# Attention and MLP mixer in one kernel: unread TensorE products in three places, token mixing in bunches, a cast moved, the last product group halved

## The chip, the cores and the metric

The kernel runs on one core of one Trainium2 chip. The metric is the device time of one execution in microseconds (us), as the median of several runs. A second source is one profiled execution of the same kernel, with its own time and its span from the first to the last instruction. The engines are TensorE (PE in the profile; its weight loads are PEld), VectorE (DVE), ScalarE (ACT), GpSimd (POOL) and SyncE (SP), which issues most of the DMAs.

## What is computed

The reference normalises queries and keys, does softmax attention over 8 batches of 12 heads (448 positions, 64 per head), joins the heads to x of 8 x 448 x 768, and sends x through an MLP mixer: first mixing along the positions, then along the channels.

```
q_n, k_n = q / (|q| + 1e-6), k / (|k| + 1e-6)
attn = softmax(q_n @ k_n.T / tau);  x = heads joined(attn @ v)
h = relu(x.T @ w_tok1) @ w_tok2          # 448 -> 256 -> 448
u = x + h.T
out = u + relu(u @ w_ch1) @ w_ch2        # 768 -> 1536 -> 768
```

## The kernel before

**Pairs of heads and slots.** The work is cut into 48 pairs of heads, six for each batch. Slot i computes the scores and exponentials of pair i, the attention output of pair i-1, and prepares pairs i+1 to i+3. The scores come in two groups of two (`score(i, 0)`, `score(i, 1)`, line 252); each of the four products of 2 x 448 columns is read by one exponential on ScalarE (line 268). `pv` (line 271) makes the attention output pO in two parts (three row tiles, then the last one), and VectorE normalises it into x16 (lines 288 and 289). Squares of q and k and their scaling to unit length run on POOL (lines 180 and 213). `norm_sum` (line 189) sums the squares on VectorE, `norm_root` (193) takes the root on ScalarE, and `norm_rec` (198) the reciprocal on VectorE.

**Opening.** The first 13 slots (`opening`, line 476) transpose q and k with TensorE (`tpose_pe`, line 233), and VectorE copies the result out (line 248). Later slots (`slot`, line 526) use a DMA for that (`tpose_dma`). The prologue (lines 443 to 471) loads, scales and transposes pair 0. In slots 1 and 2 `w2_cast` (line 138) casts one half each of w_tok2 on ScalarE; its load is issued in the prologue. Batch 0's token mixing is done pair by pair in the opening (`tok1_pair`, `tok2_pair`, `u_pair`, lines 346 to 373).

**Mixer.** For each later batch b, `mixer(b)` returns lists of jobs: `tok1` (four jobs, line 308) with a relu on ScalarE; `tok2` (two jobs for each row tile i, line 320), whose VectorE adds (line 335) give u32; after the second job of a row tile, the tile is cast to u16 (line 339 on VectorE for odd i, line 341 on ScalarE for even i) and transposed by a DMA into uT; `ch1` (twelve jobs, line 375) with a relu on ScalarE (381); `ch2` (two jobs for each row tile, line 384), with an add on VectorE (392) and stores. Even batches have three row tiles (i = 0 to 2), odd ones four (i = 3 to 6).

**Order of the work.** Each engine runs its instructions in program order. `fill` (line 434) is called five times in a slot; each call adds a fixed credit and takes jobs off the front of a list while the credit lasts. Every six slots the list is loaded again (lines 581 to 585): token mixing of the batch just finished is merged with the ch2 jobs held over from the batch before (one ch2 after every four token jobs, then the last three), then comes ch1; the new ch2 jobs are held. For the last batch (mixer 7) there are no slots left, and the list runs straight through.

**PSUM.** All products but the scores take their banks from one ring of four (`ps`, line 65). A product waits until the reader of the bank four allocations before is done.

Of the kernel before, what the change touches and what calls it, by code (L numbers as in the profile page):

```python
# [9 lines left out]
FP32 = mybir.dt.float32  # L10
FP16 = mybir.dt.float16
AF = mybir.ActivationFunctionType
ALU = mybir.AluOpType
# [10 lines left out]
def kernel(  # L24
# [136 lines left out]
    def load(i, names="qkv"):  # L161
        b, pj = pairs[i]
        for nm in names:
            t = ld.tile([P, 2, NCH, E], FP32, name=f"{nm}l", tag=f"{nm}l")
            nc.sync.dma_start(
                out=t[:].rearrange("p g c e -> p g (c e)"),
                in_=src[nm][b, 2 * pj:2 * pj + 2].rearrange("g (p c) e -> p g (c e)", c=NCH))
            st_[i][nm] = t
# [64 lines left out]
    def tpose_pe(i, act=False, between=None):  # L233
        s = st_[i]
        s["T"] = att.tile([128, 2, S], FP16, name="qkT", tag="qkT")
        for js in ((slice(0, 1), slice(1, 2)) if act else (BOTH,)):
# [12 lines left out]
            if between and not js.start:  # L249
                between()  # L250

    def score(i, g):

        s = st_[i]
        if g == 0:
            s["p"] = att.tile([P, NCH, 2, S], FP16, name="pE", tag="pE")
            s["pS"] = {}
        for c in (2 * g, 2 * g + 1):
            pS = pss.tile([P, 2, 512], FP32, name="pS", tag="pS")
            for h in range(2):  # L260
                nc.tensor.matmul(pS[:, h, 0:S],  # L261
                                 s["T"][64 * h:64 * h + 64, 1, c * P:(c + 1) * P],
                                 s["T"][64 * h:64 * h + 64, 0, :], start=True, stop=True)
            s["pS"][c] = pS
# [6 lines left out]
    def pv(i, half):  # L271
        b, pj = pairs[i]
        s = st_[i]
        xt = x16[b // 2]
        d0 = 2 * pj * E
        ts = (3,) if half else (0, 1, 2)
        pO = ps.tile([128, len(ts), 2, E + 1], FP32, name="pO", tag="ps")
        for n, t in enumerate(ts):
            c0 = 128 * t if t < 3 else S - 128
            for h in range(2):  # L280
                for c in range(NCH):
                    nc.tensor.matmul(pO[:, n, h, :], s["p"][:, c, h, c0:c0 + 128],  # L282
                                     s["v16"][:, NCH * h + c, 0:E + 1],
                                     start=(c == 0), stop=(c == NCH - 1))
        m0, hp = (64, 64 * (b % 2)) if half else (0, 0)
        nr, t0 = 128 - m0, (3 if half else 4 * (b % 2))
        rec = att.tile([128, len(ts), 2], FP32, name="rec", tag=f"rec{half}")
        nc.vector.reciprocal(out=rec[m0:128], in_=pO[m0:128, :, :, E])  # L288
        nc.vector.tensor_tensor(  # L289
            out=xt[hp:hp + nr, t0:t0 + len(ts), d0:d0 + 2 * E].rearrange(  # L290
                "p t (h e) -> p t h e", h=2),
            in0=pO[m0:128, :, :, 0:E], in1=_bcast_free(rec[m0:128], E), op=ALU.mult)
# [4 lines left out]
    def mixer(b):  # L297
# [22 lines left out]
        def tok2(i, dh):  # L320
            def job():
                pU = ps.tile([128, DH], FP32, name="pU", tag="ps")
                for tt in range(TT):
                    if i != 3:
                        c0 = 128 * (i % 4)
                        nc.tensor.matmul(pU[:], w2t[:, tt, c0:c0 + 128],  # L326
                                         r16[b][:, tt, dh * DH:(dh + 1) * DH],
                                         start=(tt == 0), stop=(tt == TT - 1))
                    else:
                        for h in range(2):  # L330
                            nc.tensor.matmul(pU[64 * h:64 * h + 64], w2t[:, tt, S - 64:S],
                                             r16[2 * g + h][:, tt, dh * DH:(dh + 1) * DH],
                                             start=(tt == 0), stop=(tt == TT - 1))
                cols = slice(dh * DH, (dh + 1) * DH)
                nc.vector.tensor_tensor(out=u32[:, i - t0, cols], in0=pU[:], in1=xt[:, i, cols],  # L335
                                        op=ALU.add)
                if dh == NDH - 1:
                    if i % 2:
                        nc.vector.tensor_copy(out=u16[:, i - t0, :], in_=u32[:, i - t0, :])
                    else:  # L340
                        nc.scalar.copy(out=u16[:, i - t0, :], in_=u32[:, i - t0, :])  # L341
                    nc.sync.dma_start_transpose(
                        out=uT[:, :, (i - t0) * 128:(i - t0 + 1) * 128], in_=u16[:, i - t0, :])
            return 0.33, job
# [38 lines left out]

        def ch2(i, dh):
            def job():
                pF = ps.tile([128, DH], FP32, name="pF", tag="ps")
                for ct in range(CT):
                    nc.tensor.matmul(pF[:], gT[:, ct, (i - t0) * 128:(i - t0 + 1) * 128],  # L388
                                     wc2t[:, ct, dh * DH:(dh + 1) * DH],
                                     start=(ct == 0), stop=(ct == CT - 1))  # L390
                o = u32[:, i - t0, dh * DH:(dh + 1) * DH]
                nc.vector.tensor_tensor(out=o, in0=pF[:], in1=o, op=ALU.add)  # L392
                end = b == B - 1 and i == t0 + nt - 1
                if dh == NDH - 1 or end:
                    store(i, slice(dh * DH, (dh + 1) * DH) if end else slice(0, D), end)
            return 1.96, job

        def store(i, cols, end):
            if i == 3:
                parts = [(h, 64 * h, S - 64, 64) for h in range(2)]  # L400
            else:
                f0 = 128 * (i % 4)
                parts = [(e, f - f0, f, n) for f, n in f_segments(f0, f0 + 128)]
            for z, (h, m, f, n) in enumerate(parts):
                rows = out[2 * g + h].rearrange("(p c) d -> c p d", c=NCH)
                queue = nc.scalar if end and z else nc.sync
                queue.dma_start(out=rows[f // P, f % P:f % P + n, cols],
                                in_=u32[m:m + n, i - t0, cols])
# [46 lines left out]
    w2_load()  # L455
    load(3, "v")
    load(4, "v")
    squares(0, act="qk")
    for j in range(2):
        norm_sum(0, j)  # L460
# [15 lines left out]
    def opening(i):  # L476

        normalize(i + 1, False)
        score(i, 0)
        norm_sum(i + 2)  # L480
        expo(i, 0)
        expo(i, 1)
        if not i:
            v_cast(0, False)
        norm_root(i + 2)
        v_cast(i + 1, i in (2, 3, 4, 5, 7))
        squares(i + 3)
        if i in wide:
            wide[i]()
        fill()  # L490
        if i >= 1:
            pv(i - 1, 0)
            pv(i - 1, 1)
        norm_rec(i + 2)
        if i in (1, 2):
            w2_cast(i - 1)
        r_, u_, add = first[0] if first else (None,) * 3
        done = [i - 2] if 2 <= i <= NPAIR else []
        if done:
            r_(i - 2)  # L500
        fill()
        score(i, 1)
        expo(i, 2)
        expo(i, 3)
        tpose_pe(i + 1)
        if i == NPAIR:
            r_(i - 1)
            done.append(i - 1)
        for pj in done:
            u_(pj)  # L510
        if i == NPAIR + 1:
            first[0][2](NPAIR - 1, False)
        for half in (True, False):
            for pj in done:
                if half or pj != NPAIR - 1:
                    add(pj, half)
        if i == NPAIR + 2:
            w1_cast(2)
        if i == 1:
            w1_cast(0)  # L520
            w1_cast(1)
        fill()
        fill()
        fill()
# [37 lines left out]
    for i in range(N + 1):  # L562
        if i + AHEAD < N:
            load(i + AHEAD)
        if i == 2:
            first.extend(mixer(0))
        if i < N and i % (2 * NPAIR) == 0:
            xt = mix.tile([128, 7, D], FP16, name="x16", tag="x16", bufs=2)
            x16[i // (2 * NPAIR)] = xt
            nc.vector.memset(xt[64:128, 3, :], 0.0)  # L570
        if i < FIRST:
            opening(i)
        else:
            if i == FIRST:
                normalize(i + 1, False)
                tpose_dma(i + 1)
            slot(i)
        if i == NPAIR:
            spread([(1.6, lambda: None)] + first[1][:8], NPAIR)
            late, held = first[1][8:], first[2]  # L580
        elif i and i % NPAIR == 0:
            front, c1, c2 = mixer(i // NPAIR - 1)
            spread(late + merge(front, held[:-3]) + held[-3:] + c1, NPAIR)
            late = []
            held = c2
    for _, job in todo + held:
# [36 lines left out]
```

## Time and profile before

| what | value |
|---|---|
| median of 3 runs | 408.05 us (406.93 to 409.0) |
| profiled execution: time | 408.18 us |
| profiled execution: span from first to last instruction | 406.0 us |
| TensorE busy | 382.7 us (94% of the span) |
| ScalarE, VectorE, POOL busy | 261.5, 234.7, 196.2 us |
| mean granted TensorE clock | 0.994 |

The page of the profile cuts the span into 40 equal slices of 10.15 us and gives the busy share of each engine in tenths, and the clock that TensorE was granted. Another view lists instructions in order of time, with the idle time of the engine before them and what ended it. A third gives the busy time of an engine in chosen stretches. The duration of a matmul in the list contains some 0.2 us until its result is written, so the step from one matmul to the next is shorter than that. By the page, TensorE's busy time is largest in pG (ch1: 121.4 us), pF (ch2: 116.6), pO (62.8) and pS (scores: 60.3).

The slots of the opening start, by their first score product, at 8.73, 13.76, 19.37, 26.03, 30.58, 35.02, 39.46, 44.75, 49.45, 56.01, 60.69 and 64.80 us (slots 0 to 11).

### The profile page before, as it was taken

What the parts mean: (1) busy time and instruction counts of PE and PEld (TensorE: products, weight loads), DVE (VectorE), ACT (ScalarE), POOL (GpSimd) and SP (SyncE); (2) the same over time, 40 slices, a digit from 0 to 9 for tenths busy, and PEclk for the clock granted to TensorE, in tenths of its full rate; (3) what the DMA queues carried; (4) which work ended last, traced back from release to release, by engine and by line L of the source; (5) the groups of instructions that cost most, each with busy time, mean ns of one, the idle gap of its engine ahead of it and who ended that gap; (6) DMA issues with size and microseconds to landing.
All of it is one profiled execution on the core that took longest, in us unless ns stands there. A gap on an engine that the chain in (4) does not pass through costs nothing.

```text
span 406.0 us, 8998 instructions
## 1 busy us (share of the span) xinstructions
PE 382.7 (94%) x3592; PEld 219.4 (54%) x3592; DVE 234.7 (58%) x534; ACT 261.5 (64%) x451; POOL 196.2 (48%) x205
## 2 busy tenths in 40 slices
PE   2798799899999999999999999999999999999996
PEld 1465566555545555555555565555545556655453
DVE  5879978557544765467634766558644773161022
ACT  6799879865767557856687567756676665521400
POOL 3979979826544647443734655644653520000000
PEclk9999989999999999999999999999999999999999
DMA  7999999939963698529773597539972352026023
GB/s 240 260 234 213 227 293 227 242 99 190 228 135 92 160 216 203 139 79 199 225 185 101 144 189 233 131 80 191 245 157 68 78 123 84 2 61 134 0 48 109
DMA packets 97305, 63.57 MB, mean 157 GB/s; under 512 B 57520, under 2 KB 93808, under 8 KB 97264
## 3 DMA queue, kind: packets, MB, share of 16 engines
q1 hardware_dynamic: 93952, 58.14, 59.7%
q0 software_dynamic: 3184, 4.72, 6.7%
q8 instruction: 28, 0.46, 0.5%
q14 instruction: 13, 0.11, 0.1%
q10 hardware_dynamic: 128, 0.15, 0.1%
HBM read 43.38 MB, written 11.01 MB: 134 GB/s over the span
## 4 chain that ended last, share of the span: by engine, by line
PE 81%; DVE 12%; DMA 4%; ACT 2%; issue 1%; SPq 0%; DVEq 0%
PE pG L379 27%; PE pF L388 27%; PE pO L282 10%; PE pS L261 9%; PE pR L313 5%; PE pU L326 3%; DVE ssq L190 2%; DVE x L289 2%; DMA kl<-in_k_dram 1%; DVE qkT L248 1%; DVE u L370 1%; ACT pE L268 1%; DMA ql<-in_q_dram 1%; DMA w2s<-in_moe_w_tok_dram 1%; DVE u L335 1%; DVE rec L288 1%
## 5 line engine op out<-in xcount | busy, mean ns | idle before, releaser
L268 ACT ACTIVATE pE<-pS 112x896 f16<-112x896 f32 x192 | 164.8, 913 | 35.3 <-PE pS L261 34.7
L379 PE MATMUL pG<-uT,wc1t 128*128 128x384 f16 (+1 forms) x576 | 121.4, 355 | 0.0
L388 PE MATMUL pF<-wc2t,gT 128*128 128x384 f16 x672 | 116.6, 326 | 0.2
L213 POOL TENSOR_TENSOR qkn<-ql,rn 112x512 f16<-112x512 f32 x47 | 49.0, 1043 | 130.6 <-DVE rn L202 109.6
L388 PEld LDWEIGHTS <-gT 128*128 128x128 f16 x672 | 63.5, 98 | 47.0 <-issue 7.3
L381 ACT ACTIVATE gT<-pG 128x384 f16<-128x384 f32 (+1 forms) x96 | 52.4, 547 | 44.8 <-PE pG L379 43.9
L379 PEld LDWEIGHTS <-wc1t 128*128 128x128 f16 x576 | 51.6, 98 | 51.4 <-issue 11.0
L392 DVE TENSOR_TENSOR u<-pF,u 128x384 f32<-128x384 f32 x56 | 31.1, 555 | 78.0 <-PE pF L388 77.7
L261 PE MATMUL pS<-qkT 64*112 64x448 f16 x384 | 60.3, 385 | 9.8 <-DVE qkT L248 5.1
L282 PEld LDWEIGHTS <-pE 112*128 112x128 f16 x1536 | 59.0, 99 | 16.1 <-issue 5.6
L282 PE MATMUL pO<-v,pE 112*128 112x65 f16 x1536 | 62.8, 196 | 0.0
L288 DVE RECIPROCAL rec<-pO 128x6 f32<-128x6 f32 x96 | 17.5, 182 | 76.1 <-PE pO L282 75.2
L190 DVE TENSOR_REDUCE ssq<-sq 112x16 f32<-112x1024 f32 (+1 forms) x50 | 58.5, 1171 | 4.2 <-ACT sq L178 3.1
L180 POOL TENSOR_TENSOR sq<-ql 112x512 f32<-112x512 f32 x46 | 48.7, 1058 | 5.6 <-DMA ql<-in_q_dram 5.6
L213 POOL TENSOR_TENSOR qkn<-kl,rn 112x512 f16<-112x512 f32 x47 | 49.0, 1042 | 0.0
L180 POOL TENSOR_TENSOR sq<-kl 112x512 f32<-112x512 f32 x46 | 48.3, 1051 | 0.0
L289 DVE TENSOR_TENSOR x<-pO,rec 128x384 f16<-128x384 f32 x96 | 40.9, 426 | 3.3
L261 PEld LDWEIGHTS <-qkT 64*112 64x112 f16 x384 | 19.1, 128 | 35.6 <-issue 22.6
L127 DVE TENSOR_REDUCE v<-vl 112x512 f16<-112x512 f32 x40 | 25.5, 640 | 0.0
L335 DVE TENSOR_TENSOR u<-pU,x 128x384 f32<-128x384 f32 x50 | 25.4, 545 | 0.1
L341 ACT CAST u<-u 128x768 f16<-128x768 f32 x14 | 11.6, 832 | 20.9 <-DVE u L335 20.9
L194 ACT ACTIVATE ln<-ssq 112x16 f32<-112x16 f32 (+1 forms) x49 | 10.9, 222 | 17.5 <-DVE ssq L190 17.2
(43 smaller groups left out, 183.4 us busy)
## 6 DMA issues: line engine op xcount, KB each, us to landing
ql<-in_q_dram SPq DMA_DIRECT2D x48, 224.0 KB, 3.6
kl<-in_k_dram SPq DMA_DIRECT2D x48, 224.0 KB, 4.0
vl<-in_v_dram SPq DMA_DIRECT2D x48, 224.0 KB, 4.2
out_dram<-u SPq DMA_DIRECT2D x8, 336.0 KB, 3.4
wc1t<-in_moe_w_ch_dram POOLq DMA_DIRECT2D x4, 576.0 KB, 7.9
wc2t<-in_moe_w_ch_dram POOLq DMA_DIRECT2D x3, 768.0 KB, 10.1
out_dram<-u SPq DMA_DIRECT2D x8, 288.0 KB, 3.8
out_dram<-u SPq DMA_DIRECT2D x7, 240.0 KB, 3.0
```

The lines of the kernel that those rows point to most:

```text
L180: nc.gpsimd.tensor_mul(out=s["sq"][:, j], in0=a, in1=a)
L190: nc.vector.tensor_reduce(out=small(i, "ssq")[:, j], in_=st_[i]["sq"][:, j], axis=AXX.X, op=ALU.add)
L213: eng.tensor_tensor(out=t[:, j].rearrange("p c g e -> p g c e"), in0=s[nm][:], in1=_bcast_free(rn, E), op=ALU.mult)
L261: nc.tensor.matmul(pS[:, h, 0:S], s["T"][64 * h:64 * h + 64, 1, c * P:(c + 1) * P], s["T"][64 * h:64 * h + 64, 0, :], start=True, stop=True)
L268: nc.scalar.activation(out=s["p"][:, c], in_=s["pS"][c][:, :, 0:S], func=AF.Exp, scale=inv_tau)
L282: nc.tensor.matmul(pO[:, n, h, :], s["p"][:, c, h, c0:c0 + 128], s["v16"][:, NCH * h + c, 0:E + 1], start=(c == 0), stop=(c == NCH - 1))
L289: nc.vector.tensor_tensor(out=xt[hp:hp + nr, t0:t0 + len(ts), d0:d0 + 2 * E].rearrange("p t (h e) -> p t h e", h=2), in0=pO[m0:128, :, :, ...
L335: nc.vector.tensor_tensor(out=u32[:, i - t0, cols], in0=pU[:], in1=xt[:, i, cols], op=ALU.add)
L379: nc.tensor.matmul(pG[:], wc1t[:, dt, ct * 128:(ct + 1) * 128], uT[:, dt, :], start=(dt == 0), stop=(dt == DT - 1))
L381: nc.scalar.activation(out=gT[:, ct, :], in_=pG[:], func=AF.Relu)
L388: nc.tensor.matmul(pF[:], gT[:, ct, (i - t0) * 128:(i - t0 + 1) * 128], wc2t[:, ct, dh * DH:(dh + 1) * DH], start=(ct == 0), stop=(ct == C ...
L392: nc.vector.tensor_tensor(out=o, in0=pF[:], in1=o, op=ALU.add)
```

## The change

It has four parts.

1. A helper `keep_busy(n, out)` issues n TensorE products of the identity matrix with itself (repeated to the width of `out`) that nobody reads. Thirteen of 512 columns stand in the prologue ahead of pair 0's squares, four of 512 columns in slot 0 between the two score groups, and eight of 256 columns in slot 7 behind the transposes of pair 8. The last ones write columns 256 to 511 of the bank that holds the second pO of slot 7, for which pO's tile is now a whole bank.
2. `w2_cast(0)` is no longer issued in slot 1 ahead of the second score group, but behind that group's exponentials.
3. For odd batches (1, 3, 5, 7) the token jobs are no longer merged four to one with the held ch2: six token jobs, one ch2, three token jobs, one ch2, three token jobs, and the other ch2. The row casts are split anew: i = 1 and 5 on VectorE, now written as a reduce over an axis of length 1 (`recast`, line 125), all others on ScalarE.
4. The very last ch2 group (the last row tile's second half of 384 columns) is computed, added and stored in two parts of 192 columns.

```diff
+    def keep_busy(n, out):
+        cols = out.shape[-1]
+        mov = bass.AP(tensor=id16[:].tensor, offset=id16[:].offset,
+                      ap=[list(id16[:].ap)[0], [0, cols // 128], [1, 128]])
+        for _ in range(n):
+            nc.tensor.matmul(out, id16[:], mov, start=True, stop=True)
...
-        pO = ps.tile([128, len(ts), 2, E + 1], FP32, name="pO", tag="ps")
+        bank = ps.tile([128, 512], FP32, name="pO", tag="ps")
+        s["bank"] = bank
+        w = len(ts) * 2 * (E + 1)
+        pO = bank[:, 0:w].rearrange("p (t h e) -> p t h e", t=len(ts), h=2)
...
-                    if i % 2:
-                        nc.vector.tensor_copy(out=u16[:, i - t0, :], in_=u32[:, i - t0, :])
+                    if i in (1, 5):
+                        recast(u16[:, i - t0, :], u32[:, i - t0, :])
...
+                parts = 2 if end and dh == NDH - 1 else 1
+                for z in range(parts):
+                    cols = slice(dh * DH + z * DH // parts, dh * DH + (z + 1) * DH // parts)
+                    pF = ps.tile([128, DH // parts], FP32, name="pF", tag="ps")
...
     load(4, "v")
+    keep_busy(13, ps.tile([128, 512], FP32, name="pW", tag="ps")[:])
     squares(0, act="qk")
...
             pv(i - 1, 1)
+        else:
+            keep_busy(4, ps.tile([128, 512], FP32, name="pW", tag="ps")[:])
         norm_rec(i + 2)
-        if i in (1, 2):
-            w2_cast(i - 1)
+        if i == 2:
+            w2_cast(1)
...
         expo(i, 3)
+        if i == 1:
+            w2_cast(0)
         tpose_pe(i + 1)
...
         if i == NPAIR + 1:
+            keep_busy(8, st_[i - 1]["bank"][:, 256:512])
             first[0][2](NPAIR - 1, False)
...
-            spread(late + merge(front, held[:-3]) + held[-3:] + c1, NPAIR)
+            if (i // NPAIR) % 2:
+                mid = merge(front, held[:-3]) + held[-3:]
+            else:
+                mid = front[:6] + held[:1] + front[6:9] + held[1:2] + front[9:] + held[2:]
+            spread(late + mid + c1, NPAIR)
```

More of the change, by code (lines that the diff above doesn't have):

```diff
@@ L385, in job @@
             def job():
[L386 to L392, printed above, removed]
-                end = b == B - 1 and i == t0 + nt - 1
-                if dh == NDH - 1 or end:
-                    store(i, slice(dh * DH, (dh + 1) * DH) if end else slice(0, D), end)
+                end = b == B - 1 and i == t0 + nt - 1
+                parts = 2 if end and dh == NDH - 1 else 1
+                for z in range(parts):
+                    cols = slice(dh * DH + z * DH // parts, dh * DH + (z + 1) * DH // parts)
+                    pF = ps.tile([128, DH // parts], FP32, name="pF", tag="ps")
+                    for ct in range(CT):
+                        nc.tensor.matmul(pF[:], gT[:, ct, (i - t0) * 128:(i - t0 + 1) * 128],
+                                         wc2t[:, ct, cols],
+                                         start=(ct == 0), stop=(ct == CT - 1))
+                    o = u32[:, i - t0, cols]
+                    nc.vector.tensor_tensor(out=o, in0=pF[:], in1=o, op=ALU.add)
+                    if end:
+                        store(i, cols, end)
+                if dh == NDH - 1 and not end:
+                    store(i, slice(0, D), end)
             return 1.96, job
```

## The prediction

> **What bounds the kernel now.** I read the page's 40 slices first, then the chain that ended last, then TensorE's time line with the idle time before each group, then TensorE's busy time in stretches of 3.41 us. From the page, TensorE's row, its clock row, and the chain by engine:
>
> ```profile
> PE   2798799899999999999999999999999999999996
> PEclk9999989999999999999999999999999999999999
> PE 81%; DVE 12%; DMA 4%; ACT 2%; issue 1%; SPq 0%; DVEq 0%
> ```
>
> From slice 9 on TensorE is full: what leaves its queue there shortens the kernel one for one, and what shortens the opening shifts all that follows. So I look for TensorE's gaps and for its slow stretches. The stretches (time, TensorE's busy us, instructions, granted clock, DMA):
>
> ```profile
> core 0: us, PE busy (x), PEclk, DMA share, GB/s
> 19.12:22.54 3.42, 2.98 (x37) 1.00 1.10 298
> 22.54:25.95 3.41, 3.41 (x29) 1.00 1.14 249
> 25.95:29.36 3.41, 3.14 (x56) 1.00 0.73 172
> 29.36:32.78 3.42, 2.59 (x49) 1.00 1.08 221
> 46.43:49.84 3.41, 1.59 (x16) 1.00 1.24 268
> 49.84:53.25 3.41, 3.41 (x35) 0.52 1.12 224
> 53.25:56.67 3.42, 3.12 (x39) 0.98 1.11 319
> ```
>
> I laid the borders so that one falls at 25.95, where durations drop, and kept the step at 3.41. The step fits: the clock is 0.52 in exactly one stretch, after the one with 47% busy (1.59 of 3.41), and is back after a stretch at 100%. A stretch of 76% (2.59) did not lower it. The clock row says 1.00 before 25.95, but durations do not: the 32 pO products take 1.94 us at 14.69 and 20.73 and 1.15 from 26.56 on, and eight transposes take 0.93 and then 0.57. So TensorE runs at about half speed until 25.95 and again from 49.84 to 53.25. The lines for the first gap, the second gap, and an odd mixer:
>
> ```profile
> 14.69 1.94 PE L282 MATMUL pO<-v,pE 112*128 112x65 f16 x32
> 17.51 0.99 ACT L139 CAST w2t<-w2s 128x448 f16<-128x448 f32 x1 [1.01 <-DMA w2s<-in_moe_w_tok_dram]
> 18.40 3.35 ACT L268 ACTIVATE pE<-pS 112x896 f16<-112x896 f32 x4
> 24.24 1.04 POOL L213 TENSOR_TENSOR qkn<-ql,rn 112x512 f16<-112x512 f32 x1 [1.31 <-DVE rn L202]
> ...
> 47.29 0.57 PE L240 MATMUL pT<-id,qkn 112*128 112x112 f16 x8
> 49.45 0.63 PE L261 MATMUL pS<-qkT 64*112 64x448 f16 x4 [1.59 <-DVE qkT L248]
> 50.02 2.10 PE L379 MATMUL pG<-uT,wc1t 128*128 128x384 f16 x6
> ...
> 179.53 1.37 DVE L339 CAST u<-u 128x768 f16<-128x768 f32 x1
> 182.38 1.15 PE L326 MATMUL pU<-r,w2t 128*128 128x384 f16 x6
> 183.56 0.56 DVE L289 TENSOR_TENSOR x<-pO,rec 128x384 f16<-128x384 f32 x1
> 184.18 0.50 PE L326 MATMUL pU<-r,w2t 128*128 128x384 f16 x2 [0.65 <-DVE x L289]
> ```
>
> **Part 1, opening, slots 0 to 3 (products, and the w2 cast moved).** A warm 128x512 product costs 0.215 us (12 of pG in a step of 2.58, 104.32 to 106.90); cold about 0.42, since six 384-column products take 1.89 us cold (50.02 to 51.91) and 0.98 warm. Thirteen of them start when id16 is written (1.32) and end at 4.2 if all are warm, at 6.8 if all are cold. The first transposes go at 6.52: at most 0.4 late. In slot 0 four more (0.87 warm, 1.7 cold) go between the two score groups, where TensorE sits from about 9.7 to 10.36. Cold, they put the second scores at about 11.4; ScalarE takes their exponentials only at 12.06, behind norm_root. The transposes of pair 1 would then end near 13.6, where VectorE copies at 13.14: at most 0.5 late. Slot 1 starts at 13.76 either way, since VectorE sets it (two v casts, norm_rec, the copy), so warm products gain nothing before it.
>
> Slot 1, warm: pO takes 1.15 for 1.94, so the second scores start at about 15.45 instead of 16.56, and their exponentials could start at 16.35, behind norm_root. Today w2_cast(0) stands ahead of them, waiting 1.01 for its DMA, and they start at 18.40. The move puts it behind them: two exponentials to 18.05, the cast to 19.04, slot 2's exponentials at 19.04 where they now start at about 20.1. The move alone, cold, would give 0.2 (scores at 16.56, exponentials 17.2 to 18.9, cast to 19.9); the clock alone nothing, the DMA's landing at 17.5 being the limit; together about 1.0. What the cast feeds, tok2_pair(0), runs at 25.1 and is not late. In slot 2 TensorE's pO, pR, scores, transposes and pU lose another 2.5 us of work, and the next exponentials come at about 24.9 instead of 26.48 (1.6), limited by ScalarE. POOL's idle time is the ceiling: 1.31 at 24.24 and 1.00 at 30.02, so 2.3. From slot 3 on ScalarE is full and carries the shift. I take **1.3**: 1.0 if the clock falls back in slot 1, whose stretch holds some 65% when warm, 1.6 if not. Ends: -0.9 (both lateness terms, nothing won) and +2.3.
>
> **Part 2, eight products of 256 columns before slot 8.** TensorE has nothing from 47.86 to 49.45, waiting for VectorE's copy of qkT. Eight products of about 0.108 us are 0.87 us; cold 1.7, which would make slot 8 0.15 late. They write columns 256 to 511 of the bank of pv's second pO. If they must wait for VectorE to read that pO (till 48.23), they end at 49.1, still inside the gap. They raise the stretch 46.43 to 49.84 from 1.59 to 2.46 of 3.41, 72%: near the 76% that held, far from the 47% that did not. If the clock holds, slot 8 (49.45 to 56.01, 6.56 us) becomes like slot 9 (56.01 to 60.69, 4.68): **1.8**, a little under the difference. Next late is VectorE's copy, then POOL (4.16 a slot). Ends: -0.2 and +2.4 (a slot of 4.11 like slot 10).
>
> The Trainium skill, "TensorE: Matmul & The Clock Gate", section "Why this matters for your kernels", speaks against this part: only idle gaps above about 3 us bring the clock down. The gap here is 1.59 us, and the clock row after it says 0.52, so the measurement decides against that rule. By the rule the eight products would change nothing and the sum would be 1.8 less.
>
> **Part 3, the mixers.** I took each group's distance to the next, less its number times its warm step, from 75 us to the end. Excess turns up in mixers 3 and 5 alone, alike: 0.21, 0.27, 0.83 and 0.13, that is 1.44 each, and 0.22 in mixer 1. The even mixers and mixer 7 run without gaps. The cause is VectorE's queue: adds of rows 3, the cast of 1.37 us (POOL running; 0.56 otherwise), adds of rows 4, pF's add and ssq (1.2) stand ahead of pv's normalisation, so the ring of four PSUM buffers is not freed and tok2 waits. The new order puts the two tok2 of rows 3 half a slot earlier, ahead of a ch2, and rows 3's cast goes to ScalarE (0.83), which is idle 5.25 of 14.7 us there. Following the credits: scores, 2 tok1, pO, 2 tok1, scores, 2 tok2, ch2, pO, 1 tok2; scores, 2 tok2, ch2, pO, scores, 3 tok2, ch2. The first two waits go. At the third place VectorE still has pF's add (to 181.5), ssq (182.65) and rec and x (183.4) ahead, and ch2 would start there at 183.45, where it now starts at 184.64: 1.2 for each of mixers 3 and 5. Mixer 7, with no attention beside it, now runs tok2 right behind tok1: the relu of the last tok1 ends 0.53 us after its products, the first tok2 covers 0.38, so 0.2 is lost. Row casts of i=1 and 5 as a reduce: about 0.94 us each (w1t's 128x768 row), for 0.56 or 1.37; VectorE has room in the even mixers. The four tok2 transposes keep four ch2 (7.8 us) of cover; SP meets the first one earlier, ahead of tpose_dma, whose input comes later anyway. Sum **2.3**. Ends: +3.1 (2 x 1.44 + 0.22) and -0.5, if the waits only move and the new one in mixer 7 doubles.
>
> **Part 4, last group halved.** The same 12 x 384 columns go as 24 products of 192; weight loads keep up (pO: 36 ns per load and 65-column product). VectorE's last add is 0.56 now for 384; with 0.29 for 128 columns (L289) 192 come to about 0.36. The first half's add and store lie under the second half's products. **0.2**; the last stores carry half the bytes, at most 0.4 more; at worst -0.2, if two more DMA issues delay the last.
>
> **Sum.** The profiled run took 408.18 with a span of 406.0. 408.18 - 1.3 - 1.8 - 2.3 - 0.2 = **402.6**. The median of the runs is 408.05, 0.13 away, so nothing is added. About 0.5% (2.04 us) can be told from no change.
>
> **Rivals.** (a) The clock doesn't follow: 72% is not enough, or the early products find no full stretch. For it: never was a stretch between 47% and 76% seen, and the stretches' place against the start may differ in each execution. Against it: 76% held. Part 2 gives 0 and part 1 0.3: 405.4; if only part 2 fails, 404.4. (b) The mixers gain nothing: ssq still stands ahead of pv's normalisation, and the ring makes another product wait as long. For it: that queue order stays. Against it: VectorE loses 1.37 us just there. 404.9. (c) Slower: the cast of rows 3 on ScalarE waits for VectorE's add and holds the exponentials behind it. The cast at 181.87 waited 1.94 and takes 0.83, so 2.77 in each of mixers 1, 3 and 5, 8.3 in all. It decides once VectorE's add ends later than the two exponentials ahead of the cast (1.72 us). Against it: the add comes 1.3 us after those scores. 408.18 + 8.3 - 3.3 = 413.2. (d) Nothing measurable: the products run cold and late (part 1 at -0.9, part 2 at -0.2) and the mixers win 1: about 408.
>
> **Chances.** Forecast 0.50, own range 400.4 to 403.8; (a) 0.25; (b) 0.13; (c) 0.04; (d) 0.08. The range 400.4 to 406.0 reaches over (a) and (b) and leaves out (c), (d) and the far ends. Faster by over 0.5%: the first three, less their upper edge, 0.86; within 0.5%: 0.09; slower: 0.05.
>
> **What would show it.** Part 1: 32 pO products of pair 0 in 1.15, not 1.94; w2_cast(0) without the wait; fourth slot's scores near 29 instead of 30.58. Part 2: no clock of 0.5 behind slot 7, and a slot 8 of about 4.7. Part 3: tok2 of mixers 3 and 5 with waits below 0.4. Part 4: a last add of 0.36. It is wrong if the clock falls in another slot, or if L341's casts wait longer and the exponentials behind them reach TensorE.

## The result, and the profile after

The changed kernel takes 402.29 us (median of 6 runs, 401.38 to 403.49) and the one before 407.49 us beside it (median of 6). The ratio is 0.9854, with a 95% interval of 0.9825 to 0.9884: 1.5% faster (the two medians alone differ by 5.2 us, 1.3%). The prediction said 402.6 us. The profiled execution after took 403.49 us with a span of 401.4 us, the highest of its six; before it was 408.18 and 406.0. Three disturbed executions are left out of the ratios, medians and ranges below: 413.38 of the kernel before, timed beside experiments 1 to 4, 410.22 in experiment 6 (its profiled one) and 414.82 in experiment 9.

From the page of the changed kernel, the same three lines as before: TensorE's busy tenths, its clock, and the chain that ended last by engine.

```profile
PE   6778899899999999999999999999999999999996
PEclk9889999999999999999999999999999999999999
PE 80%; DVE 8%; POOL 4%; ACT 3%; DMA 3%; issue 2%; SPq 0%; POOLq 0%
```

The first slice went from 2 to 6, since thirteen products stand there. The clock row dips in slices 2 and 3 (10 to 30 us) and no longer in slice 6 (51 to 61 us). VectorE's share of the chain fell from 12% to 8%.

TensorE's busy time in stretches of 3.41 us, with the borders laid on the falls of the clock of this execution (stretch; length, busy us, instructions; clock; DMA):

```profile
11.36:14.77 3.41, 1.77 (x23) 1.00 0.90 221
14.77:18.18 3.41, 3.25 (x41) 0.50 0.93 270
18.18:21.60 3.42, 2.87 (x52) 1.00 1.10 288
21.60:25.01 3.41, 1.50 (x18) 1.00 1.13 258
25.01:28.42 3.41, 3.41 (x46) 0.50 1.63 265
45.49:48.90 3.41, 2.64 (x32) 1.00 1.11 233
48.90:52.31 3.41, 3.41 (x53) 1.00 1.01 197
```

The pattern of before repeats: a stretch that TensorE fills about half (1.77, 1.50) is followed by one at clock 0.50. The stretch ahead of slot 8 now holds 2.64 us of work, and the clock stays up behind it. But the clock now falls twice earlier on.

From the list in order of time, the places that the prediction named (start, duration, engine, line, operation; in brackets the idle time before and what ended it):

```profile
14.49 1.74 PE L293 MATMUL pO<-v,pE 112*128 112x65 f16 x32
16.82 1.72 ACT L276 ACTIVATE pE<-pS 112x896 f16<-112x896 f32 x2 [0.33 <-PE pS L269]
18.43 1.01 ACT L139 CAST w2t<-w2s 128x448 f16<-128x448 f32 x1
25.20 1.94 PE L293 MATMUL pO<-v,pE 112*128 112x65 f16 x32
...
47.66 1.03 PE L258 MATMUL pO<-id 128*128 128x256 f16 x8 [0.43 <-DVE x L300]
48.82 0.63 PE L269 MATMUL pS<-qkT 64*112 64x448 f16 x4
49.39 1.15 PE L390 MATMUL pG<-uT,wc1t 128*128 128x384 f16 x6
...
180.36 1.15 PE L337 MATMUL pU<-r,w2t 128*128 128x384 f16 x6
181.04 0.56 DVE L300 TENSOR_TENSOR x<-pO,rec 128x384 f16<-128x384 f32 x1
181.66 2.12 PE L403 MATMUL pF<-wc2t,gT 128*128 128x384 f16 x12
...
397.05 0.36 DVE L407 TENSOR_TENSOR u<-pF,u 128x192 f32<-128x192 f32 x1 [0.36 <-PE pF L403]
398.04 0.36 DVE L407 TENSOR_TENSOR u<-pF,u 128x192 f32<-128x192 f32 x1 [0.63 <-PE pF L403]
```

In the opening, slot 1's second exponentials run at 16.82 instead of 18.40 and the moved cast waits for nothing; but slot 1's pO is half cold (1.74) and slot 3's pO quite cold (1.94, where it took 1.15 before). In slot 7 the eight products wait 0.43 for VectorE's reading of pO, as priced, and end before slot 8's scores; the six pG products behind them take 1.15, not 2.10. In mixer 3 the tok2 products run through, and ch2 waits for x instead: six products of 0.1625 us from 180.36 end their steps at 181.34, and pF starts at 181.66, 0.32 later. The last add takes 0.36 instead of 0.56.

Setting landmarks of the two traces side by side tells where the 4.6 us of span come from:

| landmark | before | after | earlier by | gained on the way |
|---|---|---|---|---|
| slot 3 starts | 26.03 | 24.00 | 2.03 | 2.03 |
| slot 7 starts | 44.75 | 44.12 | 0.63 | -1.40 |
| slot 9 starts | 56.01 | 53.84 | 2.17 | 1.54 |
| slot 14 starts | 83.23 | 81.48 | 1.75 | -0.42 |
| behind mixer 3's tok2 (score) | 186.92 | 183.95 | 2.97 | 1.22 |
| behind mixer 5's tok2 (score) | 279.47 | 275.32 | 4.15 | 1.18 |
| the last add starts | 402.03 | 398.04 | 3.99 | -0.16 |
| end of the span | 406.0 | 401.4 | 4.6 | 0.6 |

### The profile page after: what moved, and what is told of

Same layout as the page of the kernel before. It is cut to its first block, busy times and chain, and to the rows that moved or that the text cites. A ratio compares the mean times of both kernels' runs of the same rounds, so it can differ in the third digit from the quotient of the medians.

```text
span 401.4 us, 9080 instructions
## 1 busy us (share of the span) xinstructions
PE 383.8 (96%) x3629; PEld 220.2 (55%) x3629; DVE 232.8 (58%) x531; ACT 263.9 (66%) x455; POOL 194.6 (48%) x205
## 4 chain that ended last, share of the span: by engine, by line
PE 80%; DVE 8%; POOL 4%; ACT 3%; DMA 3%; issue 2%; SPq 0%; POOLq 0%
PE pF L403 28%; PE pG L390 25%; PE pO L293 9%; PE pS L269 9%; PE pR L324 4%; PE pU L337 3%; DVE ssq L190 3%; POOL qkn L213 2%; POOL sq L180 2%; DMA qkT<-qkn 2%; ACT pE L276 2%; DVE x L300 1%; DVE u L381 1%; DMA kl<-in_k_dram 1%; PE pU L342 1%
## 5 line engine op out<-in xcount | busy, mean ns | idle before, releaser
L403 PE MATMUL pF<-wc2t,gT 128*128 128x384 f16 (+1 forms) x684 | 116.7, 324 | 0.4
L407 DVE TENSOR_TENSOR u<-pF,u 128x384 f32<-128x384 f32 (+1 forms) x57 | 31.3, 550 | 69.2 <-PE pF L403 69.1
L269 PE MATMUL pS<-qkT 64*112 64x448 f16 x384 | 58.6, 376 | 8.4 <-DVE qkT L248 4.0
L293 PEld LDWEIGHTS <-pE 112*128 112x128 f16 x1536 | 58.1, 99 | 15.4 <-issue 4.8
L180 POOL TENSOR_TENSOR sq<-ql 112x512 f32<-112x512 f32 x46 | 47.8, 1038 | 5.5 <-DMA ql<-in_q_dram 5.5
L352 ACT CAST u<-u 128x768 f16<-128x768 f32 x18 | 15.0, 832 | 15.7 <-DVE u L346 15.7
```

The costliest lines, as they stand in the source:

```text
L180: nc.gpsimd.tensor_mul(out=s["sq"][:, j], in0=a, in1=a)
L269: nc.tensor.matmul(pS[:, h, 0:S], s["T"][64 * h:64 * h + 64, 1, c * P:(c + 1) * P], s["T"][64 * h:64 * h + 64, 0, :], start=True, stop=True)
```

## The experiments

The theory after the result had three parts. The clock of TensorE is judged over stretches of about 3.41 us, falls behind one that is about half empty, and the borders lie elsewhere in each execution, so unread products gain where they fill such a stretch. The mixers gain because VectorE's queue frees the PSUM ring earlier. The opening, once TensorE is up, meets another limit. The rivals: the falls belong to places in the program; the gain is that of the moved cast alone; the casts, not the order, help the mixers.

Each experiment is timed beside the kernel before, whose medians were 408.08 (first four), 407.99 (next four) and 408.36 us (last four).

**1. Part 3 alone.** The kernel before with the new order of the odd mixers and the new split of the casts.

```diff
-                    if i % 2:
-                        nc.vector.tensor_copy(out=u16[:, i - t0, :], in_=u32[:, i - t0, :])
+                    if i in (1, 5):
+                        recast(u16[:, i - t0, :], u32[:, i - t0, :])
...
-            spread(late + merge(front, held[:-3]) + held[-3:] + c1, NPAIR)
+            if (i // NPAIR) % 2:
+                mid = merge(front, held[:-3]) + held[-3:]
+            else:
+                mid = front[:6] + held[:1] + front[6:9] + held[1:2] + front[9:] + held[2:]
+            spread(late + mid + c1, NPAIR)
```

> The kernel before with part 3 alone (the order of the odd mixers and the split of the row casts). Theory, that part 3 takes waits off VectorE's queue and is independent of the opening: mixers 3 and 5 lose 1.44 us of waiting each and keep about 0.32, mixer 7 adds 0.13, mixer 1 adds 0.1, so 2.0 us less than before, about 0.5%. Rival, that mixers 3 and 5 gain only because the shorter opening shifts their loads and stores: the waits of 0.83 and the cast of 1.37 us stay or come back elsewhere, and the time is the one before within 0.5 us.

Measured: 406.62 us, ratio 0.9951 (0.9923 to 0.998), which is 2.0 us (0.8 to 3.1; the medians differ by 1.5). In its trace the waits of 0.21, 0.27, 0.83 and 0.13 are gone in mixers 3 and 5, and one of 0.31 and 0.33 stands in their place, in mixer 1 one of 0.33. The gain does not need the shorter opening; the rival falls.

**2. Parts 1 and 2 alone.** The changed kernel with mixers, casts and last group as before.

> The kernel before with parts 1 and 2 alone (the 13, 4 and 8 unread products and the moved w2 cast). Theory: slot 9 starts 2.2 us earlier, as with the whole change, mixer 1 gives 0.4 back to a late transpose DMA, and the time is 1.8 us less. Rival, that the shift is lost where TensorE is full: slot 9 is 2.2 us earlier, but the end is less than 1 us earlier. The clock should fall once or twice in slots 1 to 4 and not after slot 7.

Measured: 405.7 us, ratio 0.9942 (0.9917 to 0.9968), 2.4 us. Slot 9 starts at 53.76, 2.25 us earlier. In that trace slot 13 then takes 9.91 us, where the kernel before takes 8.72, because the scores of slot 14 wait 1.12 us for a transpose DMA of q and k; the 1.05 us that are left at slot 14 reach the last add (400.97, 1.06 earlier). So the stages in which TensorE is full carry the shift, but the late transpose took 1.2 us of it, three times what was expected. The parts add: 0.49% and 0.58%, and 0.15% for the 0.6 us of the last group, make 1.22%, inside the interval of the whole change (1.16% to 1.75%), near its lower end.

**3. Without the eight products.**

```diff
-            keep_busy(8, st_[i - 1]["bank"][:, 256:512])
```

> The changed kernel without the eight products of slot 7. Theory, that a stretch of 3.41 us with a busy share under about half brings the clock down: the stretch before slot 8 falls to between 47% and 55% busy, the clock of about 0.5 comes back after it, slot 8 takes 6.5 us instead of 5.0, and the kernel is 1.5 us slower than the changed one. Rival, that the early products or the shift alone keep the clock up there: slot 8 stays at 5.0 and the time is the changed kernel's.

Measured: 403.17 us, ratio 0.9874 (0.9835 to 0.9913); against 0.9854 for the changed kernel that is not told apart. In its profiled execution slot 8 took 5.02 us and the clock stayed up there: the expectation missed. The borders, found from a fall at 13.23 and a rise at 23.5, lay so that the gap was shared by two stretches. This one execution cannot tell places from borders.

**4. Without the early products.**

```diff
-    keep_busy(13, ps.tile([128, 512], FP32, name="pW", tag="ps")[:])
...
-        else:
-            keep_busy(4, ps.tile([128, 512], FP32, name="pW", tag="ps")[:])
```

> The changed kernel without the 13 products of the prologue and the 4 of slot 0. Theory, that the early products and the moved cast gain together and the cast alone little: slot 3 starts at about 25.8 us instead of 24.0, and slot 7 at 44.6 instead of 44.1, so 0.4 to 0.8 us slower than the changed kernel. Rival, that the moved cast makes the whole gain of the opening: slot 7 at 44.1 and the time the changed kernel's within 0.3 us.

Measured: 403.29 us, ratio 0.9892 (0.985 to 0.9934); the interval holds the changed kernel's ratio too. Its profiled execution missed the expectation the other way: slot 3 started at 24.97, but then no fall came at all, and slot 7 started at 43.59, before the 44.12 of the changed kernel. One trace of one execution cannot price the early products. The mean clock recorded for its four runs is 1.000 for those of 403.05 to 403.33 us and 0.992 for the one of 405.24.

**5. The changed kernel again.**

> The changed kernel itself once more, for its spread and another look at where the clock falls. Theory, that the clock is judged over stretches of 3.41 us whose borders lie elsewhere in each execution: the falls of the clock sit at other times than 14.65 and 24.89 (other by an offset that is the same for both), each behind a stretch of less than 1.95 us busy; the time is 1.3% to 1.5% under the one before. Rival, that the falls belong to places in the program: they come back within 0.3 us of where they were.

Measured: 402.31 us, ratio 0.9852 (0.9822 to 0.9881). The falls sat at 14.42 and 24.66, 0.35 from those of the first trace (14.77 and 25.01 by the clock column; the expectation had read them 0.12 too early). By this run alone the rival (places) can hardly be told from the theory, since 0.35 is just past its 0.3 and both falls moved alike. The other traces decide. The remainder of the border's time by 3.413 us was 2.2 in the kernel before, 1.1 and 0.8 in the two of the changed kernel, 3.0 in experiment 3, and 1.3 and 1.6 in experiments 8 and 11 further down. So borders do move from one execution to the next, and the two executions of the changed kernel happened to lie close.

**6. Without any unread product.** The changed kernel without all 25.

> The changed kernel without any of the 25 unread products. Theory, that they are worth what the places of the borders leave of it: 1.5 us for the eight in the executions in which the stretch before slot 8 would be under half busy, some 0.5 us for the early ones: 1 to 2 us slower than the changed kernel. Rival, that they are worth nothing and the moved cast, the mixers and the halved group make the whole gain: within 0.5 us of the changed kernel.

Measured: 404.9 us, ratio 0.9924 (0.9895 to 0.9952), on the same chip as experiment 5: 2.6 us slower than the changed kernel, more than the 1 to 2 us expected, and its eleven runs reach from 402.64 to 408.47 where the changed kernel's six lay between 401.62 and 402.99. The best of its runs come near the changed kernel's. The mean clock recorded for each run goes with its time: 1.000 in the three runs of 402.64 to 403.24 us, 0.996 at 404.02, 0.992 in the six of 404.50 to 405.71 and 0.987 at 408.47 (one stretch of 3.41 us at half clock takes 0.004 off the mean). So the products take away bad cases, and the rival falls. In the kernel before, whose waits differ too, clock and time go together less well: beside experiments 9 to 12 it took 407.53 and 409.10 us at 1.000, 409.33 and 409.34 at 0.987. The profiled execution of this experiment (410.22 us) shows one bad case, on which the difference does not rest (stretches around slot 8, same columns as above):

```profile
45.90:49.31 3.41, 1.75 (x30) 1.00 0.66 47
49.31:52.72 3.41, 2.39 (x8) 0.50 1.13 271
52.72:56.14 3.42, 0.00 (x0) 0.50 1.18 166
56.14:59.55 3.41, 3.24 (x38) 0.50 1.07 361
59.55:62.97 3.42, 3.42 (x54) 1.00 0.68 223
```

A stretch half empty, the clock down, and then a DMA (the transpose of u, 4.45 us of waiting in that trace) keeps TensorE empty, so that the clock comes back only after a stretch that is nearly full (3.24 of 3.41 us).

**7. More products, in the two gaps behind which the clock fell.**

```diff
         tpose_pe(i + 1)
+        if i in (0, 2):
+            keep_busy(4, ps.tile([128, 512], FP32, name="pW", tag="ps")[:])
```

> The changed kernel with four more unread products of 512 columns behind the transposes of slot 0 and four behind those of slot 2, where TensorE waits 1.3 and 1.2 us. Theory, that the falls of the clock after 11.2 to 14.7 and 21.5 to 24.9 come from these two gaps: no fall in the opening, slot 4 starts near 28.7 instead of 29.95, and the time is about 1 us under the changed kernel. Rival, that POOL and ScalarE bound the opening whatever the clock does: slot 7 starts at 44 again and the time is the changed kernel's.

Measured: 402.14 us, ratio 0.9852 (0.9823 to 0.9881): the changed kernel's time. Both sides were partly right. The clock fell nowhere, slot 4 started at 28.58 and slot 7 at 42.76, 2.0 us before the kernel before. Then slot 8 took 6.19 us at full clock, and slot 9 started at 53.66. What took the gain is in the list of that trace:

```profile
47.47 0.63 PE L269 MATMUL pS<-qkT 64*112 64x448 f16 x4
48.03 0.82 PE L390 MATMUL pG<-uT,wc1t 128*128 128x384 f16 x4
49.47 0.32 PE L390 MATMUL pG<-uT,wc1t 128*128 128x384 f16 x1 [0.62 <-DMA uT<-u]
50.03 0.32 PE L390 MATMUL pG<-uT,wc1t 128*128 128x384 f16 x1 [0.24 <-DMA uT<-u]
```

The fifth and sixth product of ch1 wait for the last transposes of u, which in the stretch from 38 to 54 us landed a median of 6.5 us after their issue, beside loads with medians of 8.5 to 8.7. Between 36 and 52 us the medians were 5.0 and 6.5 to 6.9 in the kernel before, 4.3 and 5.9 to 7.5 in the changed one (over the whole kernel before 3.9 and about 4). An early opening does not have to meet this: in experiments 8 and 11, with slot 7 at 42.51 and 42.64, slot 8 took 5.01 and 5.02 us and slot 9 started at 52.23 and 52.36 (in experiment 8 the transposes landed after a median of 4.0). Why they were late in experiment 7 and not in those two is not shown.

**8. The old casts.** The changed kernel with odd row tiles cast by a plain copy on VectorE again.

> The changed kernel with the row casts split as before (odd rows by a plain copy on VectorE, even rows on ScalarE). Theory, that both the order and the split are needed, since rows 3's cast (1.37 us with POOL running) stands on VectorE ahead of pv's normalisation: the waits of mixers 3 and 5 come back in part, 0.5 to 1.0 us in each instead of 0.32. Rival, that the order alone makes the gain: waits of 0.3 to 0.4 us.

Measured, one execution: 401.43 us; the waits of mixers 3 and 5 are 0.33 and 0.32, those of the changed kernel. The cast of rows 3 stands ahead of pv's normalisation as before, but takes 0.56 now (from 172.32 in that trace), not 1.37: it runs half a slot earlier, when POOL is idle (until 173.34). The order alone takes these waits away; the split of the casts does nothing to them.

**9. The moved cast alone.** The kernel before with

```diff
-        if i in (1, 2):
-            w2_cast(i - 1)
+        if i == 2:
+            w2_cast(1)
...
         expo(i, 3)
+        if i == 1:
+            w2_cast(0)
```

> The kernel before with the w2 cast moved and nothing else. Theory, that the move gains only with a faster clock: the cold scores of slot 1's second group come at 16.6 and the cast still ends near 19.9, so slot 2's second half and slot 7 start 0.2 us earlier and the time is the one before within 0.5 us. Rival, that the move is the gain of the opening and the 17 early products only hold the clock in some executions: slot 7 at about 43.6 to 44.1 instead of 44.75, 0.7 to 1.1 us less than before.

Measured: 408.41 us, ratio 1.0015 (0.9981 to 1.005), and slot 7 at 44.90. The move alone wins nothing that the runs can tell. Slot 3 did start earlier, at 24.84, but the clock fell at 25.6 and again at 49.4.

**10. The eight products alone.** The kernel before with the bank tile and the eight products.

> The kernel before with the eight products of slot 7 and nothing else. Theory, that the stretch before slot 8 is always over 60% busy with them, and often under 55% without: slot 8 takes 5.0 us in the profile, and the runs are 0.5 to 1.5 us below those of before, with fewer of them far above the median. Rival, that the eight only matter together with the early products: slot 8 at 6.5 us, the time the one before.

Measured: 407.06 us, ratio 0.9967 (0.9948 to 0.9985), 1.3 us. No fall behind slot 7, but slot 8 took 6.01 us in the profiled execution (408.1, one of the highest of its twelve), with waits of 0.30 and 0.36 for uT: as in experiment 7, a held clock meets the late transposes. The theory's size held for the median and missed for that slot.

**11. The last group whole.** The changed kernel with `parts = 1`.

> The changed kernel with the last ch2 group in one piece again. Theory: from the last product's end to the span's end 4.0 us instead of 3.4 (0.2 for an add of 0.56 instead of 0.36, the rest for the stores of 384 columns). Rival, that only the add counts and the stores land as late as with half the bytes: 3.6 us.

Measured, one execution: 402.23 us. From the start of the last add to the end of the span: 4.07 us with the group whole, 3.97 in the kernel before, 3.99 in experiment 1; halved 3.36, 3.39 and 3.35 in the changed kernel, its repetition and experiment 7. The gain is 0.6 us, and 0.4 of it is in the stores: the rival falls.

**12. A load moved out of the way.** Experiment 7, with the loads of pair 11 issued at the end of slot 6, behind the transposes of u.

```diff
-        if i + AHEAD < N:
+        if i + AHEAD < N and i != NPAIR:
             load(i + AHEAD)
...
             opening(i)
+            if i == NPAIR:
+                load(i + AHEAD)
```

> The changed kernel with the two extra groups of four products in slots 0 and 2, and the loads of pair 11 issued at the end of slot 6 instead of at its start, behind the transposes of u. Theory, that the 1.2 us that the extra products won are lost in slot 8 to transposes of u that land late behind those loads: the waits for uT (0.62 and 0.24) go, slot 9 starts at 52.5 instead of 53.66, and the time is 0.8 to 1.2 us under the changed kernel, near 401.3. Rival, that DMAs are full there and another transfer is late instead (the loads themselves, the weights): slot 9 or a later slot gives the same time back, and the time is 402.2.

Measured: 404.66 us, ratio 0.9908 (0.9881 to 0.9935), slower than the changed kernel. The waits for uT are gone and slot 8 took 5.01 us, as the theory had it; but slot 9 then took 6.11, for POOL waited for the load that had been put later:

```profile
53.97 1.04 POOL L180 TENSOR_TENSOR sq<-kl 112x512 f32<-112x512 f32 x1 [2.92 <-DMA kl<-in_k_dram]
```

The rival was right for this transfer: put back, it was the next to be late. Whether another could be put back without loss was not tried. No version tried is faster than the changed kernel beyond what the runs can tell.

## Why the prediction was right, point by point

**Which parts count, and the time.** All four parts gained, and the sum of 5.6 us stands against 4.7 in the profiled executions (408.18 to 403.49) and 5.2 in the medians. The signs and the order of the parts were right; three sizes were off and partly cancelled. By the pair of traces from which it was worked out, the sum is 0.9 us too large (403.49 measured); that the median of 402.29 lies 0.3 from 402.6 is in part luck, since the profiled execution was the slowest of its six.

**Part 1: 1.3 predicted, 0.63 in the trace.** The chain up to slot 3 was right and a little small: exponentials of slot 1 at 16.82 (16.35 predicted), slot 3 earlier by 2.03 (1.6 for its exponentials). The step that failed is "From slot 3 on ScalarE is full and carries the shift". The clock fell at 25.01, a place that the prediction had considered only for slot 1, and slot 3 took 5.95 us, of which ScalarE was busy for 4.94. The chain that ended last runs there through TensorE's cold products, from 24.81 to 29.27, and then through VectorE's copy. So the prediction's own sign, "It is wrong if the clock falls in another slot", came: the time was right, and the working of part 1 from slot 3 on was not. Of its other signs, the cast without its wait came; pO of pair 0 took 1.74 us, not 1.15, and slot 4 started at 29.95, not near 29. With the gap in slot 2 filled (experiment 7) slot 3 took 4.61, ScalarE was busy for 4.58 of it, and slot 7 started 2.0 us earlier. But the engine that carries the shift is not shown to be ScalarE: the chain of that trace runs from 26.05 to 41.30 through VectorE alone, as it does in the kernel before from 25.35 to 49.41, and both engines are nearly full (VectorE 4.24, ScalarE 4.41 of the 4.44 us of slot 5). A fall in slots 1 and 2 is cheap: in experiments 8 and 11 the clock was low from 15 to about 22 us, and slot 7 still started at 42.51 and 42.64; slot 3 started at 23.80 and 23.97 there, and at 23.97 in experiment 7 without any fall.

The 0.63 us are one pair of traces. The same opening stands in experiments 2, 5, 8 and 11 (slot 7 at 44.04, 44.00, 42.51 and 42.64 beside 44.12), the old one in experiments 1 and 10 (45.86 and 45.22 beside 44.75). No pair of these gives less than 0.63, and their means differ by 1.8 us.

**Part 2: 1.8 predicted, 1.54 in the trace.** The gap, the wait for VectorE (end 48.7 in the gap that now ends at 48.82) and the busy share (2.64 of 3.41, 72% predicted, 77% seen) came as worked out. What was missing: the fall is not sure without the products. Among the fourteen profiled executions, the eight with the products show no fall behind slot 7; of the six without, four do (before, experiments 1, 6 and 9) and two do not (3 and 4). "Next late is VectorE's copy, then POOL" was incomplete: in experiments 7 and 10 it was the transposes of u, in experiments 8 and 11 it was not.

**The rule on idle gaps.** In the kernel before, the clock fell behind a gap of 1.59 us. The longest gap ahead of any of the 18 falls in the fourteen traces, up to the last products of the kernel, was 1.93 us (experiment 10), and filling the stretch kept the clock up. The prediction had set aside for its row the rule of the Trainium skill ("TensorE: Matmul & The Clock Gate", "Why this matters for your kernels") to leave no gaps above about 3 us between bursts of products; that only such gaps bring the clock down was its own reading of that rule. The runs agree with the row: keeping to the rule was not enough here.

**Part 3: 2.3 predicted, 2.2 to 2.0 measured.** 1.22 and 1.18 for mixers 3 and 5 against 1.2 each, mixer 7 -0.16 against -0.2, and experiment 1 alone 2.0. The residual wait of 0.32 is the one named, pF behind x behind ssq. One step of the reasoning was idle: "rows 3's cast goes to ScalarE" is not needed (experiment 8); the order alone removes the waits, and shortens the cast too.

**A loss outside the four parts.** The changed kernel's trace lost 0.42 us at slot 14, where the scores waited 0.36 for a transpose DMA of q and k. This goes with the earlier opening: in the nine traces whose slot 13 starts before 74 us, the scores of slot 14 waited in seven, 0.06 to 1.12 us, and slot 13 took up to 9.91 us; in the five that start it later, none waited, and slot 13 took 8.72. The prediction had no term for it.

**Part 4: 0.2 predicted, 0.6 measured.** The add came as worked out (0.36). The stores of half the bytes end some 0.4 us sooner, which the prediction kept as the far end.

**The rivals.** (a) is true in part, as an event of single executions and not of the kernel. (b), (c) and (d) did not come. ScalarE's casts wait 15.7 us for VectorE's adds in the whole trace, less than the 20.9 of before.

**What stays open.** How much the early products win by themselves: with the kernel's other parts in place, leaving them out (experiment 4) is not told apart. The moved cast was run alone and with all early products, and the early products were not run without the move. Why transposes land late in some executions and not in others. And how far the time of the changed kernel still depends on the borders: its twelve runs lie within 401.38 and 403.49.

## What to carry to other kernels

Lay the busy time of TensorE out in stretches of the length that the clock's falls show, and look for stretches that are half empty; products that nobody reads, put in a gap where TensorE would wait anyway, keep the clock up at little cost, and their worth shows in the spread of the runs more than in one trace. When several engines feed one ring of buffers, ask which instruction stands ahead of the one that frees the buffer; moving two short jobs half a slot earlier took 2.4 us of waits away with no work removed. Before a gain in a prologue is counted, look at the time that its DMAs take to land: here a faster opening met late transposes in several traces, and gave part of its gain back. And compare several traces of each kernel before a stage is priced: slot 7 moved by up to 1.6 us between traces of one and the same opening.

## What the runs showed of the hardware

- In the fourteen traces the changes of the clock column lie multiples of 3.41 us apart: in the opening the clock stays low for 3.41, 6.83 or 10.24 us, and from a rise to the next fall it takes 3.41, 6.83, 10.24, 20.48 or 23.89 us.
- Up to the last products of the kernel the clock fell behind stretches of 3.41 us with 1.07 to 2.13 us of busy time, 17 times of 18 under 1.85, and held behind all with more than 2.2. Between 1.6 and 2.2 both happened (it held behind 1.73 from 4.53 us in the changed kernel, and behind 1.61 at the end of experiment 7), so the busy time that the profile shows is not the whole rule.
- It rose behind stretches of 3.16 us or more and, in the prologue of experiments 2 and 5, behind 2.71 and 2.81, where the step from one unread product to the next went from 0.43 to 0.22 us at 4.2 us. It stayed low behind 2.98 in the kernel before (19.12 to 22.54). So here, too, the busy time is not the whole rule.
- The clock column reads 1.00 until the first fall, though the 32 pO products there take 1.94 us: at the start the durations tell the clock, and the column does not.
- A copy of 128x768 from 32 to 16 bits on VectorE took 0.56 us while POOL was idle, and 0.57 to 1.37 beside POOL's work (1.04 in mixers 2, 4 and 6 and 1.37 in mixers 3 and 5 of the kernel before); as a reduce over an axis of length 1 it took 0.95 each time, with POOL busy or idle.
- Halving the bytes of the last stores brought their end forward by about 0.4 us.
